# A long convolution on one Trainium2 core: its transform of 64 by 64 points becomes one of 128 by 32

## The chip, the cores and the metric

The kernel runs on one core of a Trainium2 chip. The core has a matrix engine (TensorE, PE in the profile) that multiplies a stationary tile of up to 128 by 128 values, loaded by an LDWEIGHTS instruction, with a moving tile, and writes to PSUM; three engines for elementwise work (VectorE or DVE, ScalarE or ACT, GpSimd or POOL), a queue of its own for most transfers (SyncE or SP), and 16 DMA engines. The metric is the device time of one execution in microseconds.

## The reference

```python
def _A_ref(q, k, v, shift_k, ssm_k, ssm_D):       # S = 2048 rows, D = 640 channels
    ...
    kv = k_shift * v                              # k_shift: causal convolution of k with 4 taps
    ...
    y_f = kv_f * kf_f                             # spectra of kv and ssm_k, 4096 points per channel
    y = irfft(y_f)[:S] + kv * ssm_D
    return q * y
...
sa, ca, ga, sb, cb, gb = (silu(c) @ w_mod)        # six rows of 640
h = layernorm(x) * (1 + ca) + sa
x = x + ga * _A_ref(h, A_k, A_v, A_shift_k, A_ssm_k, A_ssm_D)
h = layernorm(x) * (1 + cb) + sb
x = x + gb * (relu(h @ w1 + b1) ** 2 @ w2 + b2)   # w1: 640 x 1728
return x
```

All data is float32. `irfft` above stands for the reference's inverse real transform.

## The kernel before

The work has two phases. In the first, the channels are taken in five blocks of 128 (`b` = 0 to 4), and each block's causal convolution of 2048 rows is done as a real transform of 4096 points on TensorE. In the second, the rows are taken in eight chunks of 256 (`n`), and each goes through the two dense layers, 14 strips (`f`) of `w1` and `w2` at a time, in three products of split float32 values (`mlp_front`, `mlp_back`).

One block of the first phase is staged like this.

- `kv_k`, `kv_s`, `kv_v`, `kv_m` turn k and v by TensorE transposes, apply the taps on DVE, multiply, and store the product to a DRAM tile `kv_d`. `load_h` and `load_x` bring `ssm_k` and `kv_d` back as `p`, with the position in the long row split over partitions and columns, in runs of 64 values.
- `unit_a` (eight calls a block: four for the filter, four for the data) is the first stage of the transform. Each call issues 32 matmuls, each with a stationary tile of 64 by 64 values out of `p` and 64 moving columns of the constant `cw`; four such tiles fit the array side by side. ACT moves the result to `a`.
- `spectrum` is the second stage: stationary tiles of 128 by 64 out of the constant `gb`, 128 moving columns (channels) of `a`. `front` calls it for the filter (`h`; for the first block ahead of time by `early_h`, as `eh`) and for the data (`x`); DVE multiplies the two spectra into `MS`, and POOL subtracts and adds the real products into `WS`.
- `back` is the first stage of the inverse: stationary tiles of 64 by 128 out of `gi`, 128 moving columns of `WS`, two matmuls summed in PSUM (`qp`); ACT moves it to `q`.
- `unit_t` transposes `q` (128 by 128 each, `t`), and `unit_y` is the last stage: stationary tiles of 128 by 64 out of the transposed data, 64 moving columns of the constant `ca` (`y`).
- `prep_a` (ACT), `prep_m` (DVE, times the row `row1`) and `prep_p` (POOL, plus `row0`) make the gate from the layer norm; `gate`, `finish_near` and `finish_add` apply it and store the new x to `x1_d`.

A float32 matmul of these stages is executed as two passes, each a pair of LDWEIGHTS and MATMUL; a transpose is one pair. So `unit_a`'s 1280 matmuls stand as 2560 in the profile.

The order is written out by hand. Slots `FS(b, j)` (10 a block, for `front` and `back`) and `GS(b, s)` (18 a block, for `unit_t`, `unit_y` and the next block's `unit_a`) are filled from the table `at(...)` and from `UNITS`, and `keep_order` holds every engine to the order in which the program issues its instructions. SP issues nearly all transfers in that order, with at most four outstanding (`sp_dma`, `OUT`). PSUM tiles rotate in three sets: `X` with four buffers, `Y` and `T` with two each.

Of the kernel before, what the change touches and what calls it, by code (L numbers as in the profile page):

```python
# [18 lines left out]
P = 128  # L19
# [12 lines left out]
def _constants():  # L32
    N = 4096
    n1 = np.arange(64)
    n2 = np.arange(32)
    m = np.arange(32)
    th = 2 * np.pi * ((n2[:, None] * m[None, :]) % 64) / 64
    cr, ci = np.cos(th), -np.sin(th)
    cr[:, 0] = 1.0
    ci[:, 0] = (-1.0) ** n2  # L40
    cw = np.zeros((2, 2, 32, 2, 32, 2))
    for d in range(2):
        cw[:, d, :, 0, :, d] = cr
        cw[:, d, :, 1, :, d] = ci
    cw = cw.reshape(128, 128)

    f2 = np.arange(64)
    gb = np.zeros((2, 64, 32, 2, 64))
    gi = np.zeros((2, 64, 2, 64))
    for mm in range(1, 32):  # L50
        ph = 2 * np.pi * ((n1[:, None] * (mm + 64 * f2)[None, :]) % N) / N
        c, s = np.cos(ph), np.sin(ph)
        gb[0, :, mm, 0], gb[1, :, mm, 0] = c, s
        gb[0, :, mm, 1], gb[1, :, mm, 1] = -s, c
    j = np.arange(1, 32)
    ph = 2 * np.pi * ((n1[:, None] * (64 * j)[None, :]) % N) / N
    gb[0, :, 0, 0, 1:32], gb[0, :, 0, 1, 1:32] = np.cos(ph), -np.sin(ph)
    gb[0, :, 0, 0, 0] = 1.0
    gb[0, :, 0, 1, 0] = (-1.0) ** n1
    gi[0, 1:32, 0], gi[1, 1:32, 0] = 2 * np.cos(ph).T, -2 * np.sin(ph).T  # L60
    gi[0, 0, 0] = 1.0
    gi[1, 0, 0] = (-1.0) ** n1
    i = np.arange(32)
    ph = 2 * np.pi * ((n1[:, None] * (32 + 64 * i)[None, :]) % N) / N
    gb[1, :, 0, 0, 32:], gb[1, :, 0, 1, 32:] = np.cos(ph), -np.sin(ph)
    gi[0, 32:, 1], gi[1, 32:, 1] = 2 * np.cos(ph).T, -2 * np.sin(ph).T

    ca = np.zeros((32, 2, 2, 2, 2, 2, 16, 2))
    t2 = np.arange(16)
    for h in range(2):  # L70
        nn = 2 * t2 + h
        th = 2 * np.pi * ((m[:, None] * nn[None, :]) % 64) / 64
        a, b = 2 * np.cos(th) / N, -2 * np.sin(th) / N
        a[0] = 1.0 / N
        b[0] = (-1.0) ** nn / N
        for g in range(2):
            for d in range(2):
                ca[:, g, d, 0, h, g, :, d] = a
                ca[:, g, d, 1, h, g, :, d] = b
    f = np.float32  # L80
    gb = gb.reshape(128, 16, 2, 2, 64).transpose(0, 1, 3, 2, 4)
    gt = gb.transpose(3, 4, 1, 2, 0).copy()
    gt[0, :, 0] = gi.reshape(2, 64, 128).transpose(1, 0, 2)
    return {
        "cw": cw.astype(f),
        "ca": ca.reshape(128, 256).astype(f),
        "gb": gb.reshape(128, 4096).astype(f),
        "gi": gt.reshape(128, 4096).astype(f),
    }
# [3 lines left out]
def ssm_mlp_kernel(  # L93
# [62 lines left out]
    def sub(eng, o, a, b):  # L156
# [3 lines left out]
    WX = [sb.tile([P, 10, P], F32, tag=f"WX{i}", name=f"wx{i}") for i in range(4)]  # L160
    WE = sb.tile([P, 8, P], F32, tag="WE", name="we")
    HXS = [WX[0][:, 0:4], WX[0][:, 4:8]]
    MS = [(WX[i][:, 0:4], WX[i][:, 4:8]) for i in (1, 3)]
    TS = [WX[2][:, 4 * j : 4 * j + 4] for j in range(2)]
    WS = [
        (WE[:, 0:2], WE[:, 2:4]),
        (WE[:, 4:6], WE[:, 6:8]),
        (WX[2][:, 8:10], WX[3][:, 8:10]),
        (WX[2][:, 4:6], WX[2][:, 6:8]),
    ]  # L170
    cw = WX[0][:, 8].rearrange("p (r n) -> p r n", r=2)
    ca = WX[1][:, 8:10].rearrange("p r (h n) -> p r h n", h=2)
# [21 lines left out]
    dsm = sb.tile([P, NB, DG], F32, tag="dsm", name="dsm")  # L194
# [3 lines left out]
    hsrc = ssm_k.rearrange("(g a) (n i) -> (a n) g i", a=4, i=64)  # L198
    xsrc = kv_d.rearrange("(g a) (n i) -> (a n) g i", a=4, i=64)
    pt = {}  # L200

    def p_tile(b):
        pt[b] = sb.tile([P, 2, DG, 64], F32, tag=f"S{b % 2}", name=f"p_{b}")

    def load_h(b, n=4):
        w = DG // n
        for i in range(n):
            sp_dma(
                pt[b][:, 1, i * w : (i + 1) * w],
                hsrc[:, b * DG + i * w : b * DG + (i + 1) * w, :],  # L210
            )

    def load_x(b, n=4):
        w = DG // n
        for i in range(n):
            sp_dma(
                pt[b][:, 0, i * w : (i + 1) * w],
                xsrc[:, b * DG + i * w : b * DG + (i + 1) * w, :],
            )
# [134 lines left out]
    gb = sb.tile([P, 16, 2, 2, 64], F32, tag="S5", name="gb")  # L354
    gi = sb.tile([P, 16, 2, P], F32, tag="S6", name="gi")

    def load_gi(i):
        src = gi_d.rearrange("p (g r n) -> p g r n", g=16, r=2)
        sp_dma(gi[:, 4 * i : 4 * i + 4], src[:, 4 * i : 4 * i + 4])
# [3 lines left out]
    def ab_start(b):  # L363
        AX[b] = [
            sb.tile([P, 32, P], F32, tag=f"S{2 + i}", name=f"a{i}_{b}") for i in range(2)
        ]

    def skip(b, i0=0, i1=DG):
        hd = pt[b][:, 1, i0:i1, 0]
        add(pool, hd, hd, dsm[:, b, i0:i1])  # L370

    def unit_a(b, i, q):
        t = [
            ps.tile([P, 8, 32, 2], F32, tag="X", name=f"pa_{b}_{i}_{q}_{e}", bufs=4)
            for e in range(2)
        ]
        for g in range(8):
            for e in range(2):  # L380
                l = slice(64 * e, 64 * e + 64)
                for r in range(2):
                    pe.matmul(  # L383
                        t[e][64 * r : 64 * r + 64, g].rearrange("p m d -> p (m d)"),
                        pt[b][l, i, 8 * q + g, :],
                        cw[l, r],
                        start=True,
                        stop=True,
                    )
        for e in range(2):  # L390
            c = 64 * e + 16 * q
            o = AX[b][i][:, :, c : c + 16].rearrange("p m (g d) -> p m g d", d=2)
            copy(act, o, t[e].rearrange("p g m d -> p m g d"))

    def spectrum(t, b, i, g, s):
        for r in range(2):
            for a in range(2):
                pe.matmul(  # L398
                    t[64 * a : 64 * a + 64, s + r],
                    gb[:, g, r, a],  # L400
                    AX[b][i][:, 2 * g + a],
                    start=True,
                    stop=True,
                )

    HS = {}

    def early_h(b, j):
        if j % 4 == 0:
            HS[j // 4] = sb.tile([P, 4, 4, P], F32, tag=f"XP{j // 4}", name=f"hs_{j // 4}")  # L410
        if True:
            t = ps.tile([P, 4, P], F32, tag="X", name=f"eh_{b}_{j}", bufs=4)
            spectrum(t, b, 1, 2 * j, 0)
            spectrum(t, b, 1, 2 * j + 1, 2)
            copy(act, HS[j // 4][:, j % 4], t)

    qn = [0]
    ws = {}


    def front(b, j, early):
        n = qn[0]
        qn[0] += 1
        if early:
            h = HS[j // 4][:, j % 4]
        else:
            th = ps.tile([P, 4, P], F32, tag="X", name=f"h_{b}_{j}", bufs=4)
            spectrum(th, b, 1, 2 * j, 0)
            spectrum(th, b, 1, 2 * j + 1, 2)
            h = HXS[n % 2]  # L430
            copy(act, h, th)
        tx = ps.tile([P, 4, P], F32, tag="X", name=f"x_{b}_{j}", bufs=4)
        spectrum(tx, b, 0, 2 * j, 0)
        spectrum(tx, b, 0, 2 * j + 1, 2)
        x4 = tx.rearrange("p (g r) d -> p g r d", r=2)
        h4 = h.rearrange("p (g r) d -> p g r d", r=2)
        m = [t.rearrange("p (g r) d -> p g r d", r=2) for t in MS[n % 2]]
        for r in range(2):
            mul(dve, m[r], x4, h4[:, :, r : r + 1].to_broadcast([P, 2, 2, P]))
        wr, wi = WS[n % 4]  # L440
        sub(pool, wr, m[0][:, :, 0], m[1][:, :, 1])
        add(pool, wi, m[0][:, :, 1], m[1][:, :, 0])
        if j == 0:
            pool.tensor_copy(wr[0:1, 0], m[0][0:1, 0, 0])
            pool.tensor_copy(wi[0:1, 0], m[1][0:1, 0, 1])
        ws[b, j] = (wr, wi)


    def back(b, j):
        if j == 0:  # L450
            QT[b] = sb.tile([P, DG, 32, 4], F32, tag="S4", name=f"q_{b}")
        end = b == NB - 1 and j == 3
        t = [
            ps.tile(
                [P, 4, P], F32, tag="X" if end else "Y", name=f"qp_{b}_{j}_{a}", bufs=4 if end else 2
            )
            for a in range(2)
        ]
# [26 lines left out]
    def load_xp(b):  # L485
        t = sb.tile([P, NL, P], F32, tag=f"XP{b % 2}", name=f"xp_{b}")
        src = q[:, b * P : (b + 1) * P].rearrange("(l p) d -> p l d", p=P)
        for l in range(0, NL, 4):
            sp_dma(t[:, l : l + 4], src[:, l : l + 4])
# [824 lines left out]
```

## Time and profile before

| | us |
|---|---|
| median of three runs | 690.03 |
| lowest and highest | 687.76 and 692.65 |
| span of the profiled execution | 692.6 |
| first phase in it, to the first matmul of the dense layers | about 293.6 |
| second phase in it | about 399 |

Rows of groups read: line, engine and operation, the tile written and the tile read by the program's names, partitions by elements and the count; then busy time and the mean of one instruction; then how long the engine stood idle just before such instructions, and what ended that. An idle time that is put down to "issue" is one in which the engine waited for no other engine and no data transfer that the profile shows. PE stands for matmuls, PEld for the weight loads that belong to them. Matmuls overlap, so the mean of one is longer than the step from one to the next; the step is busy time divided by count where the stream is dense.

### The profile page before, as it was taken

What the parts mean: (1) busy time and instruction counts of PE and PEld (TensorE: products, weight loads), DVE (VectorE), ACT (ScalarE), POOL (GpSimd) and SP (SyncE); (2) the same over time, 40 slices, a digit from 0 to 9 for tenths busy, and PEclk for the clock granted to TensorE, in tenths of its full rate; (3) what the DMA queues carried; (4) which work ended last, traced back from release to release, by engine and by line L of the source; (5) the groups of instructions that cost most, each with busy time, mean ns of one, the idle gap of its engine ahead of it and who ended that gap; (6) DMA issues with size and microseconds to landing.
All of it is one profiled execution on the core that took longest, in us unless ns stands there. A gap on an engine that the chain in (4) does not pass through costs nothing.

```text
span 692.6 us, 20344 instructions
## 1 busy us (share of the span) xinstructions
PE 656.1 (95%) x8741; PEld 608.5 (88%) x8741; DVE 414.1 (60%) x783; ACT 326.1 (47%) x688; POOL 255.2 (37%) x299
## 2 busy tenths in 40 slices
PE   6699789898999998999999999999999999999996
PEld 5689678797898897899999999999999999999996
DVE  4257656677787587668665564555645555555633
ACT  4426556767985995547424323333233233233221
POOL 1053155548978879553500301402203204003301
PEclk9999999999999999999999999999999999999999
DMA  9996889878772463456120020010010200200001
GB/s 235 256 255 188 226 240 271 238 209 206 198 237 65 136 185 106 134 145 210 26 77 0 1 77 1 7 71 1 38 39 1 76 2 1 77 1 0 39 1 39
DMA packets 110958, 74.72 MB, mean 108 GB/s; under 512 B 48658, under 2 KB 96146, under 8 KB 110868
## 3 DMA queue, kind: packets, MB, share of 16 engines
q1 hardware_dynamic: 108912, 72.87, 37.2%
q8 instruction: 69, 1.13, 0.7%
q10 hardware_dynamic: 1892, 0.54, 0.3%
q14 instruction: 21, 0.17, 0.1%
q0 software_dynamic: 64, 0.01, 0.0%
HBM read 58.98 MB, written 14.42 MB: 106 GB/s over the span
## 4 chain that ended last, share of the span: by engine, by line
PE 83%; DMA 5%; DVE 4%; ACT 4%; issue 2%; POOL 1%; SPq 0%; POOLq 0%; DVEq 0%; ACTq 0%
PE acc L823 27%; PE h L735 23%; PE pa L383 5%; PE qp L464 5%; PE x L398 4%; PE y L555 4%; PE h L398 3%; PE h L748 2%; PE t L544 2%; PE h L739 1%; DMA p<-kv_d 1%; PE xtp L700 1%; PE vt L276 1%; PE kt L239 1%; ACT q L146 1%
## 5 line engine op out<-in xcount | busy, mean ns | idle before, releaser
L823 PE MATMUL acc<-w_S,hring 128*128 128x320 f32 x960 | 156.7, 311 | 0.2 <-DVE hring L157 0.2
L735 PE MATMUL h<-xt,w_S 128*128 128x512 f32 (+1 forms) x770 | 149.6, 340 | 0.0
L823 PEld LDWEIGHTS acc<-w_S,hring 128*128 128x128 f32 x960 | 144.8, 188 | 4.8 <-DVE hring L157 0.7
L735 PEld LDWEIGHTS h<-xt,w_S 128*128 128x128 f32 x770 | 120.1, 189 | 14.1
L157 DVE TENSOR_TENSOR hring<-mtmp,hring 128x256 fp32r<-128x256 f32 x112 | 67.4, 601 | 69.9 <-ACT hring L146 69.9
L157 POOL TENSOR_TENSOR xt<-we,xt 128x256 fp32r<-128x256 f32 x35 | 27.5, 785 | 201.2 <-ACT xt L146 201.2
L154 DVE TENSOR_TENSOR mtmp<-h,mtmp 128x256 f32<-128x256 f32 (+1 forms) x99 | 41.9, 423 | 96.5 <-ACT mtmp L780 94.0
L780 ACT ACTIVATE mtmp<-h,b1t 128x256 f32<-128x256 f32 x91 | 43.2, 475 | 113.9 <-PE h L735 113.9
L146 ACT ACTIVATE hring<-mtmp 128x256 fp32r<-128x256 f32 x112 | 46.1, 411 | 73.9 <-DVE mtmp L782 63.2
L383 PE MATMUL pa<-wx,p 64*64 64x64 f32 x2560 | 49.4, 230 | 14.0 <-issue 7.9
L383 PEld LDWEIGHTS pa<-wx,p 64*64 64x64 f32 x2560 | 44.2, 143 | 19.9 <-issue 14.2
L146 ACT ACTIVATE a<-pa 128x512 f32<-128x512 f32 x80 | 43.1, 607 | 21.9 <-PE pa L383 21.7
L151 DVE TENSOR_TENSOR wx<-x,wx 128x512 f32<-128x512 f32 x64 | 40.8, 682 | 17.1 <-PE x L398 10.2
L555 PE MATMUL y<-wx,wx 128*64 128x64 f32 x1280 | 45.1, 225 | 4.1 <-ACT wx L146 2.5
L555 PEld LDWEIGHTS y<-wx,wx 128*64 128x64 f32 x1280 | 40.3, 138 | 8.9 <-ACT wx L146 4.0
L398 PE MATMUL x<-a,gb 128*64 128x128 f32 x640 | 42.7, 279 | 3.1 <-DVE wx L151 1.8
L782 DVE SCALAR_TENSOR_TENSOR mtmp<-mtmp 128x256 f32<-128x256 f32 x91 | 39.6, 435 | 3.1
L398 PEld LDWEIGHTS x<-a,gb 128*64 128x64 f32 x640 | 37.0, 140 | 4.5 <-PE h L398 2.5
L261 DVE SCALAR_TENSOR_TENSOR KV<-kt,tap,KV 128x511 f32<-128x511 f32 (+2 forms) x48 | 35.9, 748 | 7.5 <-ACT ktail L146 5.9
L154 POOL TENSOR_TENSOR wm<-wm,wm 128x640 f32<-128x640 f32 x20 | 32.1, 1604 | 15.9 <-ACT wm L341 15.5
L146 ACT ACTIVATE q<-qp 128x512 f32<-128x512 f32 (+1 forms) x40 | 21.3, 584 | 34.5 <-PE qp L464 34.3
L146 ACT ACTIVATE xt<-we 128x256 fp32r<-128x256 f32 x37 | 15.3, 415 | 43.4 <-DVE we L705 43.4
(152 smaller groups left out, 1117.8 us busy)
## 6 DMA issues: line engine op xcount, KB each, us to landing
wm<-in_w_mod_dram SPq DMA_DIRECT2D x25, 320.0 KB, 4.2
KV<-in_A_k_dram SPq DMA_DIRECT2D x20, 256.0 KB, 4.3
KV<-in_A_v_dram SPq DMA_DIRECT2D x20, 256.0 KB, 4.5
p<-in_A_ssm_k_dram SPq DMA_DIRECT2D x20, 256.0 KB, 4.9
p<-kv_d SPq DMA_DIRECT2D x20, 256.0 KB, 4.6
xp<-in_A_q_dram SPq DMA_DIRECT2D x20, 256.0 KB, 4.3
q<-in_A_q_dram SPq DMA_DIRECT2D x15, 320.0 KB, 5.0
out_dram<-x SPq DMA_DIRECT2D x14, 320.0 KB, 2.1
```

Source lines behind the costliest of these rows:

```text
L146: act.activation(o, i, AF.Copy)
L151: eng.tensor_mul(o, a, b)
L154: eng.tensor_add(o, a, b)
L157: eng.tensor_sub(o, a, b)
L261: dve.scalar_tensor_tensor(o, tk[:, : 512 - t], tap[:, b, t : t + 1], o, op0=ALU.mult, op1=ALU.add)
L383: pe.matmul(t[e][64 * r : 64 * r + 64, g].rearrange("p m d -> p (m d)"), pt[b][l, i, 8 * q + g, :], cw[l, r], start=True, stop=True,)
L398: pe.matmul(t[64 * a : 64 * a + 64, s + r], gb[:, g, r, a], AX[b][i][:, 2 * g + a], start=True, stop=True,)
L555: pe.matmul(y[64 * h : 64 * h + 64, 4 * (g % 2) + i].rearrange("p c l d -> p (c l d)"), tss[g][:, i, 64 * r : 64 * r + 64], ca[:, r, h], s ...
L735: pe.matmul(*x, start=(b == 0 and x is both), stop=(b == NB - 1 and x is both))
L780: act.activation(r, h[:, 1], AF.Identity, bias=b1t[:, f : f + 1])
L782: dve.scalar_tensor_tensor(r, r, 0.0, r, op0=ALU.max, op1=ALU.mult)
L823: pe.matmul(acc[2 * s + i], h[:, a, s * P : (s + 1) * P], w[:, y, i * 320 : (i + 1) * 320], start=(f == 0 and ti == 0), stop=(f == NF - 1 ...
```

## The change

The transform is split as 128 by 32 points. The number of channels in a block, the loop over blocks and the table of slots stay, with few moves.

- `p` is loaded in runs of 32 values (128 bytes) in place of 64, by `load_p`.
- `unit_a`: 64 matmuls a call in place of 32, each with a stationary tile of 64 by 32 values and 64 moving columns; eight tiles fit the array side by side. It has still eight calls a block.
- `spectrum`: 64 matmuls for each of four steps of filter and data, with stationary tiles of 64 by 32 and 64 moving columns, in place of 8 for each of eight steps. `front` becomes `front_h` (even slots) and `front_x` (odd slots).
- DVE's products in `MS` go to TensorE directly; POOL's subtractions and additions into `WS` are gone. `back` issues 128 matmuls for each of four steps, with stationary tiles of 32 by 64 (the products) and 64 moving columns of `gi`, four summed in PSUM, in place of 16.
- `unit_t`: 32 transposes a block for the last block too. `unit_y`: two matmuls of 512 moving columns for each of four calls (stationary `ca`, 128 by 64) in place of 128 matmuls of 64 columns a block.
- `prep_m`, the product with the gate's row, moves from DVE to GpSimd.
- Rows of x are laid on partitions as `(n a l)`, so `load_xp`, `q_load` and the stores of the output go in two halves of 64 partitions.
- `early_h` runs 3 steps ahead in place of 6; the tail behind the last block (`finish_near`, `stats2`) is moved into slots `GS(4, 6)` and `GS(4, 7)`.

```diff
     def unit_a(b, i, q):
...
         for g in range(8):
-            for e in range(2):
-                l = slice(64 * e, 64 * e + 64)
+            for h in range(2):
                 for r in range(2):
-                    pe.matmul(
-                        t[e][64 * r : 64 * r + 64, g].rearrange("p m d -> p (m d)"),
-                        pt[b][l, i, 8 * q + g, :],
-                        cw[l, r],
...
+                    for e in range(2):
+                        l = slice(64 * e, 64 * e + 64)
+                        o = 64 * h + 32 * r
+                        pe.matmul(
+                            t[e][o : o + 32, g],
+                            pt[b][l, i, 32 * h + 8 * q + g, :],
+                            cw[l, r],
...
-    def spectrum(t, b, i, g, s):
-        for r in range(2):
-            for a in range(2):
-                pe.matmul(
-                    t[64 * a : 64 * a + 64, s + r],
-                    gb[:, g, r, a],
-                    AX[b][i][:, 2 * g + a],
...
+    def spectrum(t, b, i, j):
+        for s in range(4):
+            for r in range(2):
+                for a in range(4):
+                    for h in range(2):
+                        l = slice(64 * h, 64 * h + 64)
+                        m = 16 * j + 4 * s + a
+                        pe.matmul(
+                            t[h][32 * a : 32 * a + 32, s, r],
+                            gb[l, m, r],
+                            AX[b][i][l, m],
...
     def back(b, j):
...
+        for s in range(4):
+            for k, (x, r, y) in enumerate(((0, 0, 0), (1, 1, 1), (0, 1, 2), (1, 0, 2))):
+                for h in range(2):
+                    w = MS[j % 2][h][x].rearrange("p (s r c) -> p s r c", s=4, r=2)
+                    for a in range(4):
+                        l = slice(32 * a, 32 * a + 32)
+                        pe.matmul(
+                            t[a][64 * h : 64 * h + 64, s],
+                            w[l, s, r],
+                            gi[l, 4 * j + s, y],
+                            start=(k == 0),
+                            stop=(k == 3),
+                        )
+        for a in range(4):
+            c = 32 * j + 8 * a
+            copy(act, QT[b][:, :, c : c + 8], t[a].rearrange("p s (r n) -> p n (s r)", r=2))
...
     def prep_m(b, j):
         uj = (UT if b < NB - 1 else UPt[b])[:, 4 * j : 4 * j + 4]
-        mul(dve, uj, uj, row1[:, b * P : (b + 1) * P].unsqueeze(1).to_broadcast([P, 4, P]))
+        mul(pool, uj, uj, row1[:, b * P : (b + 1) * P].unsqueeze(1).to_broadcast([P, 4, P]))
...
     def unit_y(b, g):
...
+        y = ps.tile([P, 4, P], F32, tag="Y", name=f"y_{b}_{g}", bufs=2)
+        for a in range(2):
+            pe.matmul(
+                y[64 * a : 64 * a + 64].rearrange("p l d -> p (l d)"),
+                ca,
+                tss[2 * g + a].rearrange("p i d -> p (i d)"),
...
```

More of the change, by code (lines that the diff above doesn't have):

```diff
@@ L66, in _constants @@
[L66 to L79, printed above, removed]
+    n1, m, f2 = np.arange(32), np.arange(64), np.arange(32)
@@ L193, in ssm_mlp_kernel, with load_p, load_h, load_x @@
     dve.memset(eps_t, EPS)
-    dsm = sb.tile([P, NB, DG], F32, tag="dsm", name="dsm")
+    dsm = sb.tile([P, NB, 64], F32, tag="dsm", name="dsm")
     tap = sb.tile([P, NB, 4], F32, tag="tap", name="tap")
-    hsrc = ssm_k.rearrange("(g a) (n i) -> (a n) g i", a=4, i=64)
-    xsrc = kv_d.rearrange("(g a) (n i) -> (a n) g i", a=4, i=64)
+    hsrc = ssm_k.rearrange("(c e) (n i) -> (e n) c i", e=2, i=32)
+    xsrc = kv_d.rearrange("(c e) (n i) -> (e n) c i", e=2, i=32)
+    qsrc = q.rearrange("(n a l) d -> a n l d", n=64, a=2)
+    osrc = out.rearrange("(n a l) d -> a n l d", n=64, a=2)
     pt = {}
     def p_tile(b):
[L203 to L219, printed above, removed]
+        pt[b] = sb.tile([P, 2, 64, 32], F32, tag=f"S{b % 2}", name=f"p_{b}")
+    def load_p(b, i, src, j):
+        c = slice(16 * j, 16 * j + 16)
+        sp_dma(pt[b][:, i, c], src[:, 64 * b + c.start : 64 * b + c.stop, :])
+    def load_h(b):
+        for j in (0, 2, 1, 3):
+            load_p(b, 1, hsrc, j)
+    def load_x(b):
+        for j in (0, 2, 1, 3):
+            load_p(b, 0, xsrc, j)
     def kv_load(i):
@@ L417, in ssm_mlp_kernel @@
[L417 to L446, printed above, removed]
+                    for e in range(2):
[5 more added lines that the diff above has]
+                            cw[l, r],
+                            start=True,
+                            stop=True,
+                        )
@@ new lines, in ssm_mlp_kernel, with spectrum_tiles, early_h @@
+    HS = {}
+    def spectrum_tiles(what, b, j):
+        return [
+            ps.tile([P, 4, 2, 64], F32, tag="X", name=f"{what}_{b}_{j}_{h}", bufs=4) for h in range(2)
+        ]
+    def early_h(b, j):
+        if j % 2 == 0:
+            HS[j // 2] = sb.tile([P, 4, 512], F32, tag=f"XP{j // 2}", name=f"hs_{j // 2}")
+        t = spectrum_tiles("eh", b, j)
+        spectrum(t, b, 1, j)
+        for h in range(2):
+            copy(act, HS[j // 2][:, j % 2 * 2 + h], t[h].rearrange("p s r c -> p (s r c)"))
@@ L449, in back @@
     def back(b, j):
         if j == 0:
[L451 to L452 removed]
+            QT[b] = sb.tile([P, 32, P], F32, tag="S4", name=f"q_{b}")
         t = [
[L454 to L457, printed above, removed]
[L458 to L470 removed]
@@ L575, in y_rest @@
-    def y_rest():
-        uo, y = ys[1]
-        dve.tensor_mul(uo[:, :, 2:], y[:, :, 2:], uo[:, :, 2:])
+        y = ps.tile([P, 4, P], F32, tag="Y", name=f"y_{b}_{g}", bufs=2)
+        for a in range(2):
+            pe.matmul(
+                y[64 * a : 64 * a + 64].rearrange("p l d -> p (l d)"),
+                ca,
+                tss[2 * g + a].rearrange("p i d -> p (i d)"),
+                start=True,
+                stop=True,
+            )
+        uo = UPt[b][:, 4 * g : 4 * g + 4]
@@ L904, in ssm_mlp_kernel @@
     load_h(1)
-    load_gi(2)
-    load_gi(3)
-    for j in range(6):
+    for j in range(3):
         early_h(0, j)
@@ L1144, in ssm_mlp_kernel @@
         for s in range(11 if last else 18):
-            if s == sy[1] and not last:
+            if s == sy[0] and not last:
                 u_tile(b)
-            for g in range(8):
+            for g in range(4):
                 if sy[g] == s:
```

307 lines of the change are left out of this document (131 added, 176 removed), and 10 rows, old and new, of the table UNITS.

## The prediction

> **What bounds the kernel now.** I read the page first, for the whole and for the transfers of instructions.
>
> ```profile
> span 692.6 us, 20344 instructions
> ...
> PE 656.1 (95%) x8741; PEld 608.5 (88%) x8741; DVE 414.1 (60%) x783; ACT 326.1 (47%) x688; POOL 255.2 (37%) x299
> ...
> q1 hardware_dynamic: 108912, 72.87, 37.2%
> q8 instruction: 69, 1.13, 0.7%
> ...
> PE 83%; DMA 5%; DVE 4%; ACT 4%; issue 2%; POOL 1%; SPq 0%; POOLq 0%; DVEq 0%; ACTq 0%
> ```
>
> TensorE is busy 95% of the span and makes 83% of the chain that ends last. The line to notice is queue q8. It moves 69 packets, 1.13 MB, so 16.4 KB each. PE executed 8741 matmuls and 8741 weight loads, 17,482 instructions; 1.13 MB over them is 65 bytes each. So q8 is, by its size, PE's own instruction stream, and one packet holds about 256 instructions, 128 pairs. The mean transfer is 0.7% of 16 engines times 692.6 us, divided by 69: 1.1 us.
>
> The next view cuts the span at three places and into its phases.
>
> ```profile
> core 0: us, PE busy (x) PEld busy (x) DVE busy (x) ACT busy (x) POOL busy (x), PEclk, DMA share, GB/s
> 34.92:89.77 54.85, 47.22 (x1140) 43.06 (x1140) 34.83 (x66) 26.40 (x51) 18.32 (x39) 0.97 0.81 224
> 89.77:135.18 45.41, 42.21 (x1013) 38.53 (x1013) 31.44 (x60) 28.39 (x54) 26.25 (x41) 1.00 0.92 252
> 129.16:135.19 6.03, 3.42 (x128) 3.12 (x128) 5.63 (x14) 2.98 (x7) 4.17 (x6) 1.00 0.84 247
> 236.08:240.36 4.28, 3.84 (x127) 3.40 (x127) 3.02 (x4) 3.62 (x9) 2.21 (x2) 1.00 0.90 244
> 0.00:293.60 293.60, 262.78 (x6176) 238.23 (x6177) 194.01 (x324) 187.65 (x377) 166.98 (x214) 0.98 0.73 200
> 293.60:692.70 399.10, 393.37 (x2568) 370.31 (x2566) 220.06 (x460) 138.50 (x312) 88.20 (x85) 1.00 0.12 40
> ```
>
> The change lies in the first phase, 293.6 us, where PE is busy 262.8 us. The dense layers (399.1 us) keep their matmuls; I leave them at nothing.
>
> Why cut at 34.9, 89.8 and 135.2? PE stops there for "issue". The order of time around the second stop, and the transfers just before:
>
> ```profile
> 83.81 1.16 PE L383 MATMUL pa<-wx,p 64*64 64x64 f32 x64 [1.65 <-DMA p<-kv_d]
> 84.90 0.66 PE L276 MATMUL vt<-ident,KV 128*128 128x128 f32 x4
> 85.49 1.66 PE L383 MATMUL pa<-wx,p 64*64 64x64 f32 x90
> 89.78 0.81 PE L383 MATMUL pa<-wx,p 64*64 64x64 f32 x38 [2.63 <-issue]
> ...
> q1 hardware_dynamic: 157, 0.31, 85.7%
> q8 instruction: 1, 0.02, 5.4%
> ```
>
> In the middle of one `unit_a` PE stands still for 2.63 us and nothing that it could wait for is late. The last two rows are of the stretch from 87.3 to 88.4 us: one packet of q8 moved in it, beside 157 of data, and PE went on about 1.4 us after. Between the first stop and the second PE executed 1140+1140 instructions, 24 short of 9 times 256; between the second and the third 1013+1013, 22 short of 8 times 256. PE's waits on semaphores, which busy counts leave out, make up such a remainder. So the stops fall on packet borders: PE runs out of instructions and waits for the next packet. Two smaller ones, 256 instructions apart, show one full cycle:
>
> ```profile
> 236.08 0.89 PEld L555 LDWEIGHTS y<-wx,wx 128*64 128x64 f32 x26 [0.50 <-issue]
> 240.36 0.72 PEld L555 LDWEIGHTS y<-wx,wx 128*64 128x64 f32 x22 [0.58 <-issue]
> ...
> q1 hardware_dynamic: 1003, 0.50, 101.1%
> ...
> q1 hardware_dynamic: 434, 0.38, 89.9%
> ```
>
> The last two rows are the stretches 236.1 to 237.95 and 239.06 to 240.36: no q8 packet moved in either, so the packet lay between them, 1.1 us. The cycle of 4.28 us is thus about 1.9 us before the transfer, 1.1 us of it, 1.3 us behind it, one packet at a time. PE cannot run faster than 256 instructions in such a cycle. Before, it seldom wants to: the first phase has 12,353 instructions and some 150 waits, 48.8 packets in 293.6 us, 6.0 us each.
>
> The Trainium skill, page "Runtime: NRT & Kernel Launch", section "Instruction fetch mechanics", says that instructions come in 16 KiB blocks of 256, that the next is fetched while the current one executes, and that crossing a block's border is mostly hidden because dispatch is slower than the fill. The trace agrees with the size of the block; the stop of 2.63 us disagrees with the rest.
>
> **The change part by part.** First TensorE's groups, as matmul records:
>
> ```profile
> L383 PE MATMUL pa<-wx,p 64*64 64x64 f32 x2560 | 49.4, 230 | 14.0 <-issue 7.9 <-DMA p<-kv_d 4.5 <-POOL p L154 1.4
> L555 PE MATMUL y<-wx,wx 128*64 128x64 f32 x1280 | 45.1, 225 | 4.1 <-ACT wx L146 2.5 <-issue 0.8 <-DVE KV L261 0.6
> L398 PE MATMUL x<-a,gb 128*64 128x128 f32 x640 | 42.7, 279 | 3.1 <-DVE wx L151 1.8 <-ACT a L146 1.1
> L398 PE MATMUL h<-a,gb 128*64 128x128 f32 x512 | 34.0, 275 | 1.3 <-ACT wx L146 1.3
> L464 PE MATMUL qp<-wx,gi 64*128 64x128 f32 x320 | 21.8, 281 | 0.8 <-POOL wx L154 0.8
> L464 PE MATMUL qp<-we,gi 64*128 64x128 f32 x320 | 20.6, 278 | 0.0
> L398 PE MATMUL eh<-a,gb 128*64 128x128 f32 x128 | 8.3, 285 | 1.3 <-ACT a L146 1.2
> ...
> 118.06 2.02 PE pa L383 x128
> 126.52 2.02 PE y L555 x64
> ```
>
> *The array's time falls.* The two last rows are of the chain: 128 records of pa take 2.02 us, 64 of y the same. A record of pa fills a quarter of the array and costs 15.8 ns, one of y half of it and 31.6 ns: 63 ns for 64 columns, divided by the tiles side by side. With eight tiles a record should cost 63/8 = 7.9 ns. After the change pa, the spectra and qp have 5120 records each (twice 512 a block): 15,360 times 7.9 is 121 us. y has 80 of 512 columns: 8 times 63 ns halved, 252 ns, is 20 us. The seven rows above sum to 222 us, so the array gains 222 - 141 = 81 us. The bounds of the new record are 7.9 ns and, if eight tiles bring no more than four, 15.8 ns, with which the array would lose 41 us.
>
> *The instructions grow.* pa gains 2560 records, the spectra 5120 - 1280 = 3840, qp 4480; y loses 1200, the transposes of the last block 32. That is 9648 more pairs, 19,296 instructions, 75.4 packets. The first phase then has 124 packets in place of 48.8. A packet of small pairs is 128 times 7.9 ns, 1.0 us of array time; its fetch takes 4. So the fetch, not the array, sets the time, and the 81 us are hidden under it.
>
> *The price of a packet* is bounded below by the parts that no load can shorten, 1.1 us of transfer and 1.3 us behind it, 2.4 us, and above by the worst block, 6.03 us between 129.16 and 135.19. The nearest row is 4.28 us, at a DMA share of 0.90. Afterwards much the same bytes are spread over some 500 us in place of 293.6, so the share falls from 0.73 to about 0.45; the wait of 1.9 us before the transfer, in which data transfers compete, should fall to about 1.5. I take 1.5+1.1+1.3 = 3.9, rounded up to 3.95 us.
>
> *The sum of the first phase.* The first small matmuls start near 10 us (8.0 us before, and a first load in shorter runs); two packets are then there. The tail's large products, half a packet, take their array time:
>
> ```profile
> 8.04 1.99 PE pa L383 x64
> ...
> L961 PE MATMUL gr<-w_gate 128*128 128x320 f32 x20 | 5.8, 438 | 0.0
> L151 DVE TENSOR_TENSOR KV<-KV,g1row 128x512 f32<-128x512 f32 x16 | 17.4, 1093 | 8.9 <-ACT KV L499 8.9
> L154 POOL TENSOR_TENSOR KV<-KV,s1row 128x512 f32<-128x512 f32 x16 | 24.1, 1524 | 5.2 <-DVE KV L151 5.2
> L157 POOL TENSOR_TENSOR we<-wx 128x256 f32<-128x256 f32 x20 | 16.2, 809 | 32.5 <-DVE wx L151 32.4
> ...
> p<-in_A_ssm_k_dram SPq DMA_DIRECT2D x20, 256.0 KB, 4.9
> p<-kv_d SPq DMA_DIRECT2D x20, 256.0 KB, 4.6
> ```
>
> I allow 9 us for gr and what surrounds it, and 5 us for waits on other engines that stick out of a packet's cycle. 10 + 121.5 times 3.95 (480) + 9 + 5 = 504 us against 293.6: 210 us more.
>
> *What lies beside it.* The gate row costs DVE 1.09 us a call and would cost POOL about 1.5 (the sum with the other row beside it), 20 calls, 30 us; four such groups of subtractions and additions as the we row, some 65 us, leave POOL, and it is busy 167 of 293.6 us already before. No cost. The filter and data loads have twice as many runs for the same bytes: between 4.9 us a load and double that. Eight loads a block are then at most 78 us of a block's 100 us: hidden by the slower TensorE; if it were as quick as before they would not be. ACT and DVE evict as many elements as before, in 100 us a block in place of 59. The new rows of x and the output move the same bytes in long runs.
>
> **The rivals.**
>
> *The fetch keeps up, and the kernel is faster.* One mechanism: the next packet is asked for earlier than I think, or several are on their way at once, so that a packet comes every 1.1 us, the transfer alone. It decides in the dense stretches, wherever a packet arrives within the array's own time for it, on average (262.8 - 81)/124 = 1.5 us. Then the array's 81 us show until the next engine binds (DVE 194 us, ACT 188, transfers 0.73 of 293.6): I give half, 40 us, so 650 us. For it: before, PE is 95% busy and the stops are few. Against it: the stops at packet borders, and that no packet of q8 moved between 239.06 us and PE's going on at 240.36. 5%. By the section on instruction fetch of the Trainium skill's page named above this is how it would go.
>
> *Eight tiles bring no more than four, and the fetch hides under it.* 15.8 ns a record is 2.0 us a packet; 690 + 41 = 731 us. It needs a fetch under 2 us and falls with it. 2%.
>
> *Every packet is as bad as the worst.* If the doubled number of data packets keeps the wait long, 5.75 us (towards 6.03): 10 + 699 + 14 = 723 us for the phase, 1120 in all. Against it the DMA share is lower. 5%.
>
> **How the numbers follow.** The profiled execution's 692.6 and 210 make 903 us; the median of the runs is 2.6 us below that execution, so 900. The forecast, that the fetch of instructions sets the first phase, has 88%. Its own range is given by the price of a packet: 3.45 us (1.05 us before the transfer, little over half of the 1.9 seen) gives 443 us for the phase and 840 in all; 4.65 us, somewhat over the measured cycle, gives 589 and 985. That leaves out the two rivals below 840, the one above and a little of the forecast's own, near 2 in 10 together. About 1% is what a measurement of this kernel can tell from no change. Faster by more: the first rival, 0.05. Within: 0.02. Slower: 0.93.
>
> **What would show it.** In the changed kernel q8 should have some 144 packets, and PE and PEld 18,389 each. PE's busy share in the first phase should fall well below half, with "issue" as the largest entry of the chain, in stops of 2 to 3 us, one every 256 instructions; a `unit_a` (64 matmuls, 256 instructions) about every 4 us. Within a packet eight-tile records should run near 8 ns each. The dense layers should take 399 us as before. A PE that is busy above 80% in the first phase, or pa waiting for ACT, POOL or a transfer in place of "issue", would make the prediction wrong.

## The result, and the profile after

The changed kernel takes 952.38 us (median of four runs, 950.99 to 958.25) against 689.7 us for the kernel before: 1.3798 times as long, with a 95% interval of 1.3737 to 1.3858. The profiled execution has a span of 950.7 us. The forecast was slower, 900 us, with a range of 840 to 985.

The page of the changed kernel, with the lines that answer to those of before (busy time of the engines; of the 40 slices TensorE, its granted clock and the DMA engines; the two large DMA queues; the chain that ended last by engine):

```profile
span 950.7 us, 39512 instructions
...
PE 738.4 (78%) x18389; PEld 650.2 (68%) x18389; DVE 384.0 (40%) x760; ACT 330.3 (35%) x728; POOL 211.2 (22%) x228
...
PE   5455764466655667566755899999999999999997
...
PEclk9665597656975587555955799999999999999999
DMA  8923089342584246203430345201010100102011
...
q1 hardware_dynamic: 147856, 72.34, 30.2%
q8 instruction: 144, 2.36, 1.1%
...
PE 74%; issue 20%; DMA 3%; DVE 1%; SPq 1%; ACT 1%; ACTq 0%; POOL 0%; DVEq 0%
```

TensorE executes 18,389 pairs, as many as were counted ahead, and its queue q8 moves 144 packets in place of 69. In the first 22 of the 40 slices, which lie in the first phase, PE is busy four to seven tenths; "issue" has grown from 2% of the chain to 20%. The DMA engines are busy for a smaller share of the longer span than before (30.2% for data, 37.2% before), although the packets are a third more.

The two phases, and within the first its middle, two short stretches with few and with many data transfers, and one cycle out of the first of these (span of the stretch, busy time and count of each engine, granted clock, DMA share, GB/s):

```profile
0.00:550.10 550.10, 344.76 (x15823) 279.91 (x15823) 163.71 (x300) 191.39 (x416) 123.15 (x143) 0.68 0.44 108
550.10:950.70 400.60, 393.63 (x2569) 370.24 (x2567) 220.26 (x461) 138.96 (x313) 88.01 (x85) 1.00 0.14 40
11.20:530.70 519.50, 321.21 (x15599) 264.23 (x15580) 151.50 (x272) 178.22 (x387) 114.46 (x125) 0.66 0.44 106
404.60:419.20 14.60, 9.23 (x512) 8.08 (x512) 2.49 (x4) 3.73 (x8) 0.52 (x1) 0.50 0.02 4
153.40:171.30 17.90, 8.45 (x517) 7.15 (x518) 2.49 (x4) 5.43 (x10) 3.17 (x6) 0.79 0.81 173
412.06:415.53 3.47, 2.37 (x128) 2.02 (x128) 0.00 (x0) 1.21 (x4) 0.00 (x0) 0.50 0.02 5
```

Nearly all of the loss lies in the first phase: 550.1 us against 293.6. The dense layers take 400.6 us against 399.1. From 11.2 to 530.7 us TensorE executed 31,179 matmuls and loads, with its waits 122 packets, 4.26 us each. Four packets took 14.6 us where almost no data moved (3.65 us each) and 17.9 us where the DMA engines were busy 0.81 (4.5 us each). The trace also has the start of every q8 packet: 122 of them start in that stretch, and of the 121 steps from one to the next, the shortest is 3.3 us, the median 3.90 us, and 19 are longer than 5 us.

In order of time, such a stretch looks like this (start, length, engine, line, tiles, count, and what ended the idle time before):

```profile
408.59 2.26 PE L447 MATMUL qp<-gi,wx 32*64 32x64 f32 x128 [1.56 <-issue]
412.06 0.51 PE L447 MATMUL qp<-gi,wx 32*64 32x64 f32 x11 [1.21 <-issue]
412.50 1.94 PE L388 MATMUL h<-a,gb 64*32 64x64 f32 x117
415.53 0.45 PE L388 MATMUL h<-a,gb 64*32 64x64 f32 x11 [1.10 <-issue]
415.69 2.01 PE L388 MATMUL x<-a,gb 64*32 64x64 f32 x116
419.20 0.45 PE L388 MATMUL x<-a,gb 64*32 64x64 f32 x12 [1.50 <-issue]
```

128 matmuls, a stop, 127 or 128 matmuls, a stop. The stops don't fall on the borders of `front_h`, `front_x` or `back`; they fall after every 256 instructions, in the middle of a group of matmuls that wait for nothing. One cycle of it by the transfers, 412.1 to 413.1 and 413.1 to 414.1 us: in the first no packet moved at all, in the second this one,

```profile
q8 instruction: 1, 0.02, 5.8%
```

and TensorE went on at 415.53. The cycle of 3.47 us is 1.1 us before the transfer, 0.9 us of it and, as it ended at 414.07, 1.5 us behind it. So the next packet is fetched while TensorE executes the current one, but it comes after the current one has run out. In this cycle the matmuls are busy 2.37 us and the weight loads 2.02 us: neither fills it.

### The profile page after: what moved, and what is told of

Its sections match the earlier page's. It is cut to its first block, busy times and chain, and to the rows that moved or that the text cites. A ratio compares the mean times of both kernels' runs of the same rounds, so it can differ in the third digit from the quotient of the medians.

```text
span 950.7 us, 39512 instructions
## 1 busy us (share of the span) xinstructions
PE 738.4 (78%) x18389; PEld 650.2 (68%) x18389; DVE 384.0 (40%) x760; ACT 330.3 (35%) x728; POOL 211.2 (22%) x228
## 2 busy tenths in 40 slices
DMA packets 149974, 75.31 MB, mean 79 GB/s; under 512 B 89777, under 2 KB 137137, under 8 KB 149810
## 3 DMA queue, kind: packets, MB, share of 16 engines
q1 hardware_dynamic: 147856, 72.34, 30.2%
## 4 chain that ended last, share of the span: by engine, by line
PE 74%; issue 20%; DMA 3%; DVE 1%; SPq 1%; ACT 1%; ACTq 0%; POOL 0%; DVEq 0%
PE acc L770 20%; PE h L682 17%; PE qp L447 10%; PE pa L369 7%; PE x L388 4%; PE h L388 4%; PE t L505 2%; PE y L512 2%; PE h L695 2%; PE h L686 1%; DMA p<-in_A_ssm_k_dram 1%; SPq L129 1%; PE kt L224 1%; DMA KV<-in_A_v_dram 1%; PE vt L261 1%
## 5 line engine op out<-in xcount | busy, mean ns | idle before, releaser
L447 PE MATMUL qp<-gi,wx 32*64 32x64 f32 x5120 | 96.7, 315 | 61.2 <-issue 56.0
L447 PEld LDWEIGHTS qp<-gi,wx 32*64 32x64 f32 x5120 | 86.0, 199 | 72.3 <-issue 65.4
L369 PE MATMUL pa<-wx,p 64*32 64x64 f32 x5120 | 77.0, 263 | 55.5 <-issue 53.1
L369 PEld LDWEIGHTS pa<-wx,p 64*32 64x32 f32 x5120 | 64.7, 123 | 70.0 <-issue 62.1
L770 PE MATMUL acc<-w_S,hring 128*128 128x320 f32 x648 | 105.4, 311 | 0.0
L770 PEld LDWEIGHTS acc<-w_S,hring 128*128 128x128 f32 x648 | 97.8, 188 | 2.8
L388 PE MATMUL x<-a,gb 64*32 64x64 f32 x2560 | 47.3, 294 | 42.2 <-issue 40.3
L388 PEld LDWEIGHTS x<-a,gb 64*32 64x32 f32 x2560 | 38.6, 138 | 47.4 <-issue 44.9
L145 POOL TENSOR_TENSOR wm<-wm,wm 128x640 f32<-128x640 f32 x20 | 30.9, 1543 | 102.9 <-ACT wm L326 102.5
L770 PE MATMUL acc<-w_S,w_WX 128*128 128x320 f32 x312 | 51.4, 312 | 0.4 <-DVE w_WX L148 0.2
L770 PEld LDWEIGHTS acc<-w_S,w_WX 128*128 128x128 f32 x312 | 47.0, 188 | 2.4 <-DVE w_WX L148 0.7
```

The source lines that it names most:

```text
L145: eng.tensor_add(o, a, b)
L369: pe.matmul(t[e][o : o + 32, g], pt[b][l, i, 32 * h + 8 * q + g, :], cw[l, r], start=True, stop=True,)
L388: pe.matmul(t[h][32 * a : 32 * a + 32, s, r], gb[l, m, r], AX[b][i][l, m], start=True, stop=True,)
L447: pe.matmul(t[a][64 * h : 64 * h + 64, s], w[l, s, r], gi[l, 4 * j + s, y], start=(k == 0), stop=(k == 3),)
L770: pe.matmul(acc[2 * s + i], h[:, a, s * P : (s + 1) * P], w[:, y, i * 320 : (i + 1) * 320], start=(f == 0 and ti == 0), stop=(f == NF - 1 ...
```

## The experiments

The theory is that TensorE's instructions, brought in packets of 256, one packet at a time, set the time of the first phase. Eleven kernels were run, each beside the kernel before on the same chip. "First phase" is the time to the first matmul of the dense layers in the profiled execution (293.2 us before; the cut at 293.6 above is a little later).

| kernel | us (median) | first phase, us | packets of q8 |
|---|---|---|---|
| before | 689.7 to 693.2 | 293.2 | 69 |
| after | 952.38 | 550.1 | 144 |
| a_cols16: after, a quarter of the columns | 952.59 | 549.6 | 144 |
| a_half: after, 2560 pairs fewer | 874.29 | 471.8 | 124 |
| b_split: before, 2560 pairs more | 768.05 | 366.7 | 89 |
| a_bigruns: after, `p` in long runs | 948.88 | 547.4 | 144 |
| a_out2: after, two transfers outstanding | 948.12 | 541.2 | 144 |
| a_quiet: after, long runs and one outstanding | 1114.58 | 677.3 | 144 |
| a_gate_dve: after, gate row on DVE | 950.39 | 547.8 | 144 |
| b_pool: before, gate row on GpSimd | 699.49 | 297.0 | 69 |
| b_sums: before, sums on TensorE | 717.25 | 318.4 | 74 |
| b_last512: before, last stage of 512 columns | 701.44 | 293.5 | 60 |
| b_last512_out8: the same, eight outstanding | 697.80 | 295.0 | 60 |

### Instructions or array time

**a_cols16** keeps every instruction and takes array work away.

```diff
-                            t[e][o : o + 32, g],
+                            t[e][o : o + 32, g, 0:16],
                             pt[b][l, i, 32 * h + 8 * q + g, :],
-                            cw[l, r],
+                            cw[l, r, 0:16],
...
-                            t[h][32 * a : 32 * a + 32, s, r],
+                            t[h][32 * a : 32 * a + 32, s, r, 0:16],
                             gb[l, m, r],
-                            AX[b][i][l, m],
+                            AX[b][i][l, m, 0:16],
```

> The changed kernel with 16 of the 64 moving columns in every matmul of unit_a and of the spectra (10,240 of the 15,360 small records); the other 48 columns are not computed, their place is filled by copies of the 16. Every instruction and every packet of q8 stays. Theory (the fetch of instructions sets the first phase): no change, 952 us within 1%, 144 packets, a packet every 4.2 us. Rival (the array's own time in the small tiles, at the lower granted clock, sets it): pa, x, h and eh are busy 169 us in the changed kernel; a quarter of the columns takes at least half of that away, so 870 us or less.

Measured: 952.59 us (two runs), the changed kernel's 952.38 within 0.1%. Its groups in the first phase, and those of the changed kernel below:

```profile
L369 PE MATMUL pa<-wx,p 64*32 64x16 f32 x5120 | 61.5, 206 | 60.7 <-issue 58.9 <-DMA p<-kv_d 1.5
L389 PE MATMUL x<-a,gb 64*32 64x16 f32 x2560 | 35.7, 217 | 47.3 <-issue 44.8 <-ACT wx L137 2.5
L389 PE MATMUL h<-a,gb 64*32 64x16 f32 x2048 | 26.6, 214 | 33.7 <-issue 33.7
```

```profile
L369 PE MATMUL pa<-wx,p 64*32 64x64 f32 x5120 | 77.0, 263 | 55.5 <-issue 53.1 <-DMA p<-kv_d 2.0 <-POOL p L145 0.4
L388 PE MATMUL x<-a,gb 64*32 64x64 f32 x2560 | 47.3, 294 | 42.2 <-issue 40.3 <-ACT a L137 1.2 <-ACT wx L137 0.7
L388 PE MATMUL h<-a,gb 64*32 64x64 f32 x2048 | 35.9, 286 | 25.4 <-issue 25.4
```

These matmuls were busy 123.8 us in place of 160.2, and the time did not move; "issue" ahead of them grew from 118.8 to 137.4 us. A quarter of the columns took away 23% of the busy time, not the half that the rival's 870 us supposed: an array that sets the time would have given some 916 us. That is excluded as well. Array time of `unit_a` and the spectra is off the path.

**a_half** takes instructions away from the changed kernel, **b_split** adds them to the kernel before, whose tiles stay 64 by 64.

```diff
-            for k, (x, r, y) in enumerate(((0, 0, 0), (1, 1, 1), (0, 1, 2), (1, 0, 2))):
+            for k, (x, r, y) in enumerate(((0, 0, 0), (0, 1, 2))):
```

> The changed kernel with two of the four matmuls of each sum in back left out (the second product of the real and of the imaginary part): 2560 fewer pairs, 20 packets fewer. Theory: 20 packets at 4.2 us, 84 us, so 868 us (860 to 880). Rival (the array's time of these records): at the 18.9 ns that a record of qp is busy 48 us, so 904; at 7.9 ns 20 us, so 932.

```diff
-                    pe.matmul(
-                        t[e][64 * r : 64 * r + 64, g].rearrange("p m d -> p (m d)"),
+                    for x in (slice(0, 32), slice(32, 64)):
+                        pe.matmul(
+                            t[e][64 * r : 64 * r + 64, g].rearrange("p m d -> p (m d)")[:, x],
                             pt[b][l, i, 8 * q + g, :],
-                        cw[l, r],
+                            cw[l, r][:, x],
```

> The kernel before with each matmul of unit_a done as two of 32 moving columns on the same 64 by 64 tile: 2560 more pairs, 5120 instructions, 20 packets, on the old layout and with the same columns. Theory: about 20 packets at 4.2 us less a little slack, 750 to 775 us, with more stops for issue in pa. Rival (small tiles of 32, eight tiles side by side or their clock cost the time, not the number of instructions): the columns are the same, 690 to 700 us.

Measured, one run each: 874.29 and 768.05 us, both inside the theory's range and outside the rivals'. The first phase changed by 78.3 us for 20 packets (3.9 us each) and by 73.5 us for 20 (3.7 us each). In a_half the group qp was busy 44.7 us less (52.0 for 96.7) and "issue" ahead of it fell by 30.9 us (25.1 for 56.0): both parts of the cycle went.

In b_split the columns and the tiles are those of before. PE's waits, and the group pa:

```profile
PE pa L384 <- issue: 24.6, 17, 2.9
PE y L556 <- issue: 6.8, 6, 2.4
PE kt L239 <- DMA KV<-in_A_k_dram: 4.4, 1, 4.4
```

```profile
L384 PE MATMUL pa<-wx,p 64*64 64x32 f32 x5120 | 100.2, 231 | 27.7 <-issue 24.6 <-DMA p<-kv_d 1.5 <-POOL p L154 1.4
```

There are 17 stops ahead of pa, where before there were 4 of 7.9 us together. But stops are the smaller part of the loss: "issue" ahead of pa and y grew by 23 us, and the busy time of pa by 51 us, from 49.4 to 100.2. Two calls of `unit_a` before (64 columns) and one in b_split (32 columns), both at a granted clock of 1.00:

```profile
117.99 2.10 PE L383 MATMUL pa<-wx,p 64*64 64x64 f32 x128
```

```profile
88.11 2.13 PE L384 MATMUL pa<-wx,p 64*64 64x32 f32 x128
```

A record of half the columns takes as long, some 16.5 ns. So the rival's price, no more than 700 us because the columns are the same, was wrong: TensorE's own time for 2560 more pairs is 51 us, or some 744 us for the run, and the 768 measured lie another 24 us above that. The run shows that twice the instructions of `unit_a` cost time with the old tiles, at a granted clock of 0.93 in the first phase for 0.98 before. It does not separate the fetch from TensorE's own time for a pair. That the fetch sets the changed kernel's time stands on a_cols16, a_half and the stops in the trace.

### What the price of a packet depends on

**a_bigruns** and **a_out2** change the data transfers alone.

```diff
-        sp_dma(pt[b][:, i, c], src[:, 64 * b + c.start : 64 * b + c.stop, :])
+        d = kv_d if src is xsrc else ssm_k
+        row = d[P * b : P * b + P].rearrange("p (c i) -> p c i", i=32)
+        sp_dma(pt[b][:, i, c], row[:, c])
```

> The changed kernel with the loads of p (from ssm_k and from kv_d) taken in runs of 2 KB in place of 128 bytes: the same bytes, in another order, so the transform is of other data; instructions on TensorE unchanged. If the small packets of these 40 loads are what lengthens the wait ahead of an instruction packet (1.2 us where few data packets move, 2.1 us where many do), the mean cycle falls from 4.2 to about 3.9 us: 920 to 935 us. If the wait does not depend on the size of the data packets: 945 to 955 us.

```diff
-OUT = 4
+OUT = 2
```

> The changed kernel with at most two of SP's transfers outstanding in place of four. If the wait ahead of an instruction packet grows with the data transfers that are under way, the cycle shortens: 925 to 945 us. If the data then comes late, which the first phase with its long cycles should bear: 955 us or more.

**a_quiet** does both, with `OUT = 1`.

> The changed kernel with both: loads of p in runs of 2 KB (other data) and one of SP's transfers outstanding in place of four. Theory (the wait ahead of an instruction packet is what the data transfers lengthen): the bound cycle falls towards the 3.7 to 3.8 us of its quiet stretches, so 122 packets save up to 45 us, 910 to 935 us, unless data comes late. Rival (the wait has another cause): 945 us or more with a cycle of 4 us or more.

Measured: 948.88 us (947.84 to 949.93), 948.12 us (945.51 to 950.73) and 1114.58 us. None of the three was run side by side with the changed kernel, only each beside the kernel before. The first lies in the rival's range: half the data packets (73,174 in place of 149,974, and 7,857 in place of 89,777 under 512 bytes) brought 0.4%, so the doubled number of runs in `load_p` is no large part of the price. The second missed both ranges, by 3 us on the side of no gain; neither difference is clear with two runs. The third is a miss: with one transfer outstanding the data came late,

```profile
PE pa L371 <- DMA p<-kv_d: 46.2, 6, 22.7
PE kt L226 <- DMA KV<-in_A_k_dram: 36.3, 8, 11.6
```

which hides what it was made to show. The starts of the q8 packets tell a little more. In a_quiet the DMA share was over 0.5 in 3 of the 122 steps (48 of 121 in the changed kernel), and the median step was 3.80 us in place of 3.90: the typical packet is hardly cheaper, and 0.1 us over 122 packets is 12 us, not the 45 that were hoped for. Within the changed kernel the 49 steps at a DMA share under 0.1 have a mean of 3.77 us and the 36 at 0.7 or more one of 4.62; but the other work differs between them too, so how much of that is due to the transfers is not shown.

### The parts of the change, one at a time

**b_pool** moves the gate row on the kernel before; **a_gate_dve** moves it back on the changed one.

```diff
-        mul(dve, uj, uj, row1[:, b * P : (b + 1) * P].unsqueeze(1).to_broadcast([P, 4, P]))
+        mul(pool, uj, uj, row1[:, b * P : (b + 1) * P].unsqueeze(1).to_broadcast([P, 4, P]))
```

> The kernel before with the gate row's product alone moved from DVE to GpSimd (20 calls, 1.09 us each on DVE, about 1.5 on GpSimd). Prediction: no cost, 690 us within 1%. Rival: GpSimd, busy 167 us of the first phase and now with 30 more, holds up the sums ahead of back: 700 us or more.

> The changed kernel with the gate row's product back on DVE. Alone on the kernel before this move cost 1.1%. If the fetch hides it in the changed kernel, as the prediction had it: 952 us within 1%. If GpSimd's added work sticks out there too: 945 us or less.

Measured: 699.49 us, 1.0109 times the kernel before (1.0078 to 1.0140), and 950.39 us. Alone the move costs 1.1%, between the two expectations and nearer to the rival's; in the changed kernel taking it back is worth 0.2%, nothing that can be told from no change. Why it is free there is not shown. The changed kernel has a first phase made long by TensorE, and its GpSimd has lost the sums ahead of `back` (123.15 us busy in the first phase with the gate row, 166.98 before without it); no run has the one without the other.

**b_sums** lets TensorE sum the real products on the old tiles.

```diff
-            for r in range(2):
+            for k, (x, r, y) in enumerate(((0, 0, 0), (1, 1, 0), (0, 1, 1), (1, 0, 1))):
...
-                        gi[l, 4 * j + u, r],
-                        w[r][l, u % 2],
+                        gi[l, 4 * j + u, y],
+                        w[x][l, u % 2, r],
```

> The kernel before with the sums of real products alone moved to TensorE, on the old tiles of 64 by 128: back issues 4 matmuls in place of 2 and reads DVE's products, POOL's subtractions and additions (about 65 us) are gone. The minus sign of the second product and the special row of the first matmuls are left out. 640 more pairs, 1280 instructions, 5 packets; qp on the array doubles, 42 us more. Theory (TensorE, array and fetch, bounds the phase before): 715 to 735 us. Rival (the step over POOL between DVE and back holds up TensorE, and its going pays for the matmuls): 700 us or less.

Measured: 717.25 us, 1.0337 times (1.0280 to 1.0393), in the theory's range; the first phase is 25.2 us longer. The step over POOL did not hold TensorE up enough to pay for 640 more pairs.

**b_last512** puts the last stage with 512 columns on the kernel before.

```diff
-                        gi[l, 4 * j + u, r],
                         w[r][l, u % 2],
+                        gi[l, 4 * j + u, r],
...
+        for k in range(2):
+            for e in range(2):
+                l = slice(64 * e, 64 * e + 64)
+                a = 2 * k + e
+                pe.matmul(
+                    y[32 * a : 32 * a + 32].rearrange("p l d -> p (l d)"),
+                    ca[l],
+                    tss[2 * g + k][l].rearrange("p i d -> p (i d)"),
```

> The kernel before with the idea of the last stage alone: the operands of back are swapped, so that the transposes put one row's 64 values on 64 partitions, and unit_y does 16 matmuls of 512 moving columns a block with a stationary tile of 64 by 32, in place of 128 of 64; first stage, spectra and POOL's sums stay as before, rows of x on partitions as four groups of 32. 1120 fewer pairs, 8.75 packets, and y on the array falls from 45 to about 10 us. Theory: fewer instructions and less array time both help where TensorE bounds the phase, 655 to 675 us. Rival (DVE, ACT or the transfers in 32 partitions bind instead): 685 us or more.

In this run the channels of a block stand in another order than in the reference.

> The last stage with 512 columns on the kernel before, with the channels' order mended, and with eight of SP's transfers outstanding in place of four. In the run with four, TensorE was busy less but waited for transfers more (p from kv_d 11.5 us). If the limit on outstanding transfers is what binds there: 665 to 685 us. If the DMA engines themselves do (busy above 80% in most of the first phase): 690 to 705 us.

Measured: 701.44 us, 1.0128 times (1.0106 to 1.0150), and 697.80 us, 1.0098 times (1.0067 to 1.0128). The rivals held in both. The first phase of b_last512 by engine, the group y in it, and its largest wait:

```profile
0.00:293.50 293.50, 249.81 (x5023) 203.74 (x5023) 190.88 (x322) 186.40 (x375) 165.32 (x214) 0.96 0.79 199
```

```profile
L536 PE MATMUL y<-wx,wx 64*32 64x512 f32 x160 | 27.4, 657 | 5.7 <-ACT wx L143 5.7
```

```profile
PE pa L382 <- DMA p<-kv_d: 11.5, 4, 6.6
```

TensorE executes 1152 pairs fewer, is busy 13 us less than before, and the phase is as long in the profiled execution (696.41 us, the fastest of five): it waits for `kv_d` and for ACT in place of working, at a DMA share of 0.79. y fell to 27.4 us, not to 10. So TensorE's instructions were not the only bound here; transfers stand close behind. They have changed as well: the same 72.87 MB keep the DMA engines busy 40.5% of the span, 37.2% before. The rows of x in groups of 32 partitions are new in them, and no run has the new last stage without that layout. No version here beats the kernel before.

## Why the prediction was right, point by point

**The mechanism** was the one forecast. The packet of 256 instructions, one on its way at a time, read from three stops in the profile of before, governs most of the changed first phase: 144 packets as counted, stops in the middle of groups, no time gained with a quarter of the columns (a_cols16), 78 us for 20 packets fewer (a_half), and, with the array's time in it, 73 us for 20 more (b_split).

Three signs that it named came out otherwise. PE's busy share of the first phase is 0.63, not well below half; the stops last 1.5 to 2.1 us on average by group, not 2 to 3 us; and "issue" is second in the chain, behind PE. All three follow from records that are longer than forecast (below) in a cycle of about the length forecast.

**The rivals** that the fetch keeps up, and that the array's time shows, fell with the same runs. The worst case for every packet did not come: 4.26 us, not 5.75.

**The sum** was short by 46 us in the first phase (504 against 550.1). Three terms:
- The packets, 480 us with 5 us for single long waits, took 519.5 us, 34.5 us more: 4.26 us each as a mean, in place of 3.95. The typical packet was priced right: 102 of the 121 steps between packets are shorter than 5 us, with a mean of 3.92. The mis-sized term is the long ones: the other 19 exceed 3.95 us by 41 us together, where 5 us had been allowed. The largest:

```profile
126.70:139.80 13.10, 9.62 (x125) 5.25 (x129) 9.09 (x23) 6.50 (x13) 2.58 (x8) 0.99 0.95 222
```

One packet took 13.1 us there, 9 us over the mean. In order of time, its end:

```profile
132.64 1.07 PE L512 MATMUL y<-wx 128*64 128x512 f32 x2 [1.44 <-ACT wx L137]
...
139.05 2.25 PE L369 MATMUL pa<-wx,p 64*32 64x64 f32 x161 [1.24 <-DMA p<-kv_d]
```

It holds transposes, y's matmuls of 512 columns and waits for ACT and `kv_d`, no stop for "issue": not the fetch set its time. Of the other long steps some hold a wait for another engine as well (4.7 us for DVE, ended at 177.5 us), and some hold small pairs alone with one long stop, such as this one:

```profile
46.75 2.11 PE L369 MATMUL pa<-wx,p 64*32 64x64 f32 x127 [4.37 <-issue]
```

What lengthens such a stop is not shown.

- The tail, 9 us, measured 19.4 (530.7 to 550.1). The 9 us were for gr and what surrounds it; the last transposes and y lie behind the last small matmuls too, and were executed at a granted clock of 0.74 (first row), which returned to 1.00 for gr (second):

```profile
530.70:543.80 13.10, 11.86 (x124) 6.93 (x124) 3.05 (x10) 6.67 (x15) 6.36 (x9) 0.74 0.56 166
543.80:550.10 6.30, 6.30 (x31) 4.75 (x31) 4.24 (x10) 3.52 (x9) 0.00 (x0) 1.00 0.01 3
```

- The start, 10 us, was right: the first small matmul starts at 9.98 us. The 519.5 us are counted from 11.2, which accounts for the last 1.2 us.

**The array's time** was wrong, and hidden. 7.9 ns a record was forecast, and busy time "well below half" of the phase; pa took 15.0 ns (77.0 us over 5120), qp 18.9, and PE was busy 344.8 of 550.1 us. A lower clock is part of it. Two whole packets of the changed kernel, the first at a granted clock of 1.00, the second at 0.50:

```profile
19.28 1.51 PE L369 MATMUL pa<-wx,p 64*32 64x64 f32 x128 [0.54 <-issue]
```

```profile
28.30 2.11 PE L388 MATMUL eh<-a,gb 64*32 64x64 f32 x128 [0.33 <-issue]
```

That is 11.8 and 16.5 ns a pair; with four tiles side by side, before, it was 16.4 at full clock (2.10 us above). So at full clock eight tiles save a little over a quarter of four's time, not the half that the prediction took from dividing 63 ns by the tiles, and at half the clock they save nothing against four at full clock; b_split shows likewise that a record does not shrink with its columns. Most of the 81 us that eight tiles were to save do not exist; a_cols16 shows that their absence costs nothing here.

**"No cost" for the gate row** was right for the changed kernel; on the kernel before the same edit costs 1.1%. The prediction's reason, that the sums leave GpSimd, was not tested apart from the long first phase. **"No cost" for twice the runs** of `p` fits a_bigruns, where runs sixteen times as long brought 0.4%, which is not clear of noise.

**The dense layers** took 400.6 us for the 399.1 that were left at nothing.

## What to carry to other kernels

Count the instructions of an engine, not only its busy time: divide them by the 256 of a packet, price a packet by a stop that no other engine explains (3.5 to 4.5 us here), and compare with the array time of the same instructions: 4 us over 128 pairs are some 30 ns a pair, and where the array needed less than that here, more pairs added time. A part of a change can cost time alone and none inside the whole: measure it on both kernels. And a part that takes work from the busiest engine can gain nothing: in b_last512, 13 us less of TensorE's work came back as waits for transfers and ACT.

## What the hardware showed that was not expected

The granted clock fell in a phase that waits for instructions. It was 0.98 in the first phase before and 0.68 after. It was 1.00 from 361.6 to 371.7 us, where TensorE was busy 9.00 of 10.1 us, and 0.50 from 371.8 to 450.2, where it was busy 49.21 of 78.4 us. The stop just before the fall lasted 1.1 us, and the longest behind it 2.9 us. The Trainium skill, page "TensorE: Matmul & The Clock Gate", section "What's actually happening", gives a clock that falls to half after an idle window of about 3.4 us; here it fell to the half that the page gives, and stayed there, with no stop that long on either side of the fall. In a_cols16, with less work for each packet, the mean over the whole execution was 0.772 against 0.812, and the time was the same.

The packet's own transfer is the smaller part of its price. Of the quiet cycle of 3.47 us, 0.9 us is the transfer of 16 KB; 1.1 us before it and 1.5 us behind it are there with no other packet moving. In three cycles of the busy stretch (157.64 to 171.26 us, by the stops and the packets' starts) the part before the transfer was 1.5, 2.2 and 2.1 us, the transfer 1.5, 1.2 and 1.1, and the part behind it 1.3 to 1.4 in all three: what grew is mostly the wait before the transfer.
